# Quarter-array products in one group per turn, selection and feed-forward as two table-driven generators with a PSUM bank each, results summed in the same turn

## The chip, the cores and the metric

One Trainium2 chip, one core of it. The metric is the device time of the program in microseconds; smaller is better. TensorE is called PE here, its weight loads PEld, VectorE DVE, ScalarE ACT, GpSimd POOL, and SyncE, which issues most of the transfers, SP.

## The reference

First a recurrence over 768 steps for 4 batches and 8 heads of 48 (`r`, `k`, `v`, `w` are fp32):

```python
for t in range(S):
    cur = np.einsum('bhd,bhe->bhde', u[None] * kt, vt)
    y[:, :, t] = np.einsum('bhd,bhde->bhe', rt, state + cur)
    state = wt[:, :, :, None] * state + np.einsum('bhd,bhe->bhde', kt, vt)
```

Then, on `x` = `y` with the heads side by side (4 x 768 x 384), in each batch the 128 rows with the highest score go through a two-layer network and are added back:

```python
scores = np.einsum('bsd,d->bs', x, w_gate)
for b in range(B):
    top_idx = np.argpartition(-scores[b], capacity)[:capacity]
    xe = x[b, top_idx]
    ye = np.maximum(xe @ w1, 0.0) @ w2          # 384 -> 1024 -> 384
    g = 1.0 / (1.0 + np.exp(-scores[b, top_idx]))
    out[b, top_idx] = x[b, top_idx] + g[:, None] * ye
```

## The kernel before

The steps of a batch are cut into 6 chunks of 128, so there are 24 chunks, numbered n = 0 to 23, and the order of all instructions is written out by hand: a loop of 28 **turns**, n = -4 to 23. Each engine runs its instructions in the order in which the code names them. A turn works on several chunks at different depths: it loads chunk n+7 (L526), takes the logarithm of `w` of chunk n+4 (`lnw`), its running sums by two 128x128 triangular matmuls (`sums`, `later_sums`), scales `k` and `r` of chunk n+3 (`scaled`), transposes chunk n+2 (`turned` for "K" and for "R"), forms the 64x64 scores and the state's growth of chunk n+1 (`scores`, `fresh`, then `masked` and `states` on DVE), and finishes chunk n (`from_state`, `from_chunk`). `result`, which adds the finished PSUM tile to `vo`, multiplies with `w_gate` and stores `x`, is called for n-1 at the start of the turn.

Two kinds of matmul alternate on PE. `from_state`, `scores`, `fresh` and `from_chunk` use quarters of the array (64 rows by 64 columns); `turned`, `sums`, `later_sums` and everything of the second part use the whole array. fp32 operands go through PE in more than one pass, so 16 quarter matmuls show as x32 in the trace.

PSUM has eight banks: four for the two tiles `ps_p` (one for even, one for odd chunks), three that rotate through `turned` K, `turned` R, `sums` and `later_sums` (pool `psR`), one for the second part (pool `psM`). `from_chunk(n)` writes columns that `from_state(n)` wrote from other rows of the array; it therefore waits for an ACT instruction that comes after `from_state`: the copy of `turned` R's bank (L317), and in the last two turns, where there is none, a small copy `seen` (L306).

The second part is one generator, `mixture(b)`, of 28 pieces: scores of the batch spread to all partitions (`ps_e`, `every`), six comparisons on DVE (`ahead`), counts by matmul (`ps_r`), `rank`, `pick`, row numbers (`ps_i`, `idx`), the gather of 128 rows of `x` from DRAM by POOL (`xe`), its transposes (`ps_x`, `xeT`), the gate, then eight pieces of the first layer (`ps_h`; after every fourth an ACT `Relu` to `hid`), eight of the second (`ps_f`), `ye` and a scatter by POOL. `mixture(b)` is begun in turn 6(b+1) and advanced by 5, 5, 5, 4, 5 and 4 pieces in that turn and the five after it (L479), at three places of each turn (L540, L549, L551). That of the last batch runs behind the loop (L553). The gather reads rows that `result` stored, so it needs the batch's last store.

`x` has three buffers, so `result(n)` waits until the store of chunk n-3 has landed. SP issues the loads, the weights of the second part (one piece per turn from turn 0 to 6), the stores and a small transfer `all` (L165) in one queue.

## Time and profile before

| | |
|---|---|
| median of 3 runs | 261.3 us (260.32 to 262.85) |
| the profiled execution's own time | 257.75 us |
| its span | 256.0 us |
| busy PE / PEld / DVE / ACT / POOL | 206.2 / 151.3 / 127.7 / 89.6 / 91.3 us |
| moved by DMA | 29.36 MB, mean 115 GB/s |
| first sums that need loaded chunk 4 (turn 0) | start at 22.5 us |
| turn 12 begins (K transposes of chunk 14) | 118.72 us |
| `x` of the last chunk | 219.14 us |

Busy time of PE is no measure of its work by itself: matmuls overlap, and one at half clock counts double. What counts is the distance from one group's start to the next group's start. Times in rows are from the span's start. The granted clock is given as a share of 2.4 GHz.

### The profile page before, as it was taken

How to read it: one execution, taken by the hardware profiler on the slowest of the kernel's cores; microseconds unless marked ns; L12 is line 12 of the kernel's file. 1: busy time of each engine (PE TensorE's matmuls, PEld its weight loads, DVE VectorE, ACT ScalarE, POOL GpSimd, SP SyncE). 2: the span in 40 equal slices, each digit the busy share in tenths (PEclk: the TensorE clock that was granted, in tenths of full speed). 3: DMA queues.
4: the chain of work that ended last, by engine and by line, in shares of the span. 5: the costliest groups of instructions: out<-in, count | busy, mean ns of one | idle time of the engine just before them, and what ended most of it. 6: DMA issues, size and time to landing. Idle time of an engine off the chain costs nothing.

```text
span 256.0 us, 8427 instructions
## 1 busy us (share of the span) xinstructions
PE 206.2 (81%) x3634; PEld 151.3 (59%) x3634; DVE 127.7 (50%) x330; ACT 89.6 (35%) x215; POOL 91.3 (36%) x113
## 2 busy tenths in 40 slices
PE   3786999869869499999878999999768999328760
PEld 1353777646646288667556876766548886117630
DVE  6471567535784075236795643437975331641010
ACT  3773465515632124543631455146311210100100
POOL 3370676324551424442655154417453120110010
PEclk9996799988995599999995999999975999955995
DMA  7998999989899974557558325001120000110001
GB/s 143 204 190 164 196 223 213 202 209 218 199 213 212 224 177 78 109 131 157 124 113 200 66 66 124 31 3 64 34 65 3 33 33 33 61 31 0 0 0 44
DMA packets 108540, 29.36 MB, mean 115 GB/s; under 512 B 103376, under 2 KB 107728, under 8 KB 108496
## 3 DMA queue, kind: packets, MB, share of 16 engines
q1 hardware_dynamic: 107984, 27.18, 48.5%
q0 software_dynamic: 512, 1.57, 2.0%
q8 instruction: 30, 0.49, 0.8%
q14 instruction: 14, 0.11, 0.2%
HBM read 23.20 MB, written 5.51 MB: 112 GB/s over the span
## 4 chain that ended last, share of the span: by engine, by line
PE 59%; DMA 13%; DVE 10%; SPq 7%; issue 6%; ACT 1%; POOL 1%; POOLq 0%; DVEq 0%; ACTq 0%
PE ps_h L443 11%; PE ps_f L453 9%; PE ps_p L310 7%; PE ps_x L152 6%; DMA out_dram<-x 6%; SPq L105 6%; PE ps_t L217 6%; PE ps_l L172 5%; PE ps_p L233 5%; DMA xe<-out_dram,idx 5%; PE ps_p L249 4%; PE ps_p L292 4%; DVE ahead L361 3%; DVE sc L261 2%; DMA w<-in_w_dram 2%
## 5 line engine op out<-in xcount | busy, mean ns | idle before, releaser
L261 DVE TENSOR_TENSOR sc<-ps_p,mask 128x512 f32<-128x512 f32 x24 | 16.6, 692 | 67.9 <-PE ps_p L249 67.9
L183 POOL TENSOR_TENSOR rk<-r,k 128x384 f32<-128x384 f32 x24 | 24.0, 998 | 52.9 <-DVE r_buf L207 52.9
L152 PE MATMUL ps_x<-lw,tri 128*128 128x384 f32 x48 | 25.6, 619 | 7.7 <-ACT lw L135 7.7
L219 ACT COPY Kt<-ps_t 128x512 f32<-128x512 f32 x24 | 14.0, 584 | 46.6 <-PE ps_t L217 42.0
L443 PE MATMUL ps_h<-xeT,w 128*128 128x128 f32 x192 | 29.0, 307 | 1.5 <-ACT hid L448 0.9
L281 POOL TENSOR_TENSOR s<-mid,all_buf 128x192 f32<-128x192 f32 x20 | 12.8, 640 | 45.6 <-issue 19.4
L310 PE MATMUL ps_p<-v,sc 64*64 64x48 f32 x768 | 29.0, 227 | 0.0
L310 PEld LDWEIGHTS ps_p<-v,sc 64*64 64x64 f32 x768 | 26.4, 143 | 4.3 <-issue 2.7
L443 PEld LDWEIGHTS ps_h<-xeT,w 128*128 128x128 f32 x192 | 26.5, 216 | 4.0 <-ACT hid L448 1.2
L453 PE MATMUL ps_f<-w,hid 128*128 128x384 f32 x64 | 24.4, 507 | 0.9 <-ACT hid L448 0.7
L184 POOL TENSOR_TENSOR rk<-rk,u_bc 128x384 f32<-128x384 f32 x24 | 24.0, 1000 | 2.7 <-DMA u_bc<-in_u_dram 0.9
L233 PE MATMUL ps_p<-Rt,Kt 48*64 48x64 f32 x768 | 18.1, 237 | 6.2 <-DVE x L326 6.2
L154 ACT ACTIVATE rise<-ps_x 128x384 f32<-128x384 f32 x24 | 11.8, 491 | 30.3 <-PE ps_x L152 26.6
L172 PE MATMUL ps_l<-lw,tri_s 128*128 128x384 f32 x48 | 22.1, 547 | 0.0
L198 POOL TENSOR_TENSOR vo<-v,own 128x384 f32<-128x384 f32 x24 | 21.2, 884 | 2.3 <-DVE x L326 2.3
L233 PEld LDWEIGHTS ps_p<-Rt,Kt 48*64 48x64 f32 x768 | 14.7, 145 | 10.9 <-DVE x L326 7.4
L249 PEld LDWEIGHTS ps_p<-v,k_buf 64*48 64x48 f32 x704 | 11.7, 130 | 13.6 <-issue 10.7
L219 ACT COPY Rt<-ps_t 128x512 f32<-128x512 f32 x24 | 14.1, 586 | 15.5 <-PE ps_t L217 15.5
L326 DVE TENSOR_TENSOR x<-ps_p,vo 128x384 f32<-128x384 f32 x24 | 13.3, 553 | 11.6 <-DMA out_dram<-x 5.8
L292 PE MATMUL ps_p<-s,Rt 48*64 48x48 f32 x704 | 17.3, 231 | 1.0 <-DVE mid L279 0.9
L361 DVE SCALAR_TENSOR_TENSOR ahead<-every,score,behind 128x768 bf16<-128x768 f32 (+5 forms) x24 | 17.5, 770 | 1.2 <-ACT every L351 1.2
L292 PEld LDWEIGHTS ps_p<-s,Rt 48*64 48x64 f32 x704 | 14.3, 143 | 5.8 <-issue 4.2
(78 smaller groups left out, 290.9 us busy)
## 6 DMA issues: line engine op xcount, KB each, us to landing
w<-in_w_dram SPq DMA_DIRECT2D x24, 192.0 KB, 4.0
k<-in_k_dram SPq DMA_DIRECT2D x24, 192.0 KB, 4.1
r<-in_r_dram SPq DMA_DIRECT2D x24, 192.0 KB, 3.9
v<-in_v_dram SPq DMA_DIRECT2D x24, 192.0 KB, 3.8
out_dram<-x SPq DMA_DIRECT2D x24, 192.0 KB, 2.8
w<-in_moe_w_dram SPq DMA_DIRECT2D x3, 512.0 KB, 5.2
w<-in_moe_w_dram SPq DMA_DIRECT2D x4, 384.0 KB, 4.8
all_buf<-line_buf SPq DMA_DIRECT2D x20, 2.0 KB, 3.2
```

Source lines behind the costliest of these rows:

```text
L152: nc.tensor.matmul(ps[:, 0:C], tri, t["lw"], start=True, stop=True)
L172: nc.tensor.matmul(ps[:, 0:C], tri_s, t.pop("lw"), start=True, stop=True)
L183: sync(nc.gpsimd.tensor_mul(rk, t.pop("r"), t.pop("k")), t["scaled"], "one port")
L184: nc.gpsimd.tensor_mul(rk, rk, u_bc)
L219: after[n - 2] = nc.scalar.copy(out=t[name + "t"], in_=ps)
L233: nc.tensor.matmul(P[half(sub), par, j * HB:(j + 1) * HB], t["Kt"][half(par, D), j, half(sub)], t["Rt"][half(par, D), j, half(sub)], start ...
L249: nc.tensor.matmul(t["P"][half(par, D), sub, SC + j * D:SC + (j + 1) * D], t["K"][half(sub), 2 * j + par, 0:D], t["v"][half(sub), 2 * j + ...
L292: nc.tensor.matmul(t["P"][half(sub), par, j * D:(j + 1) * D], t["Rt"][half(par, D), j, half(sub)], t["s1" if sub else "s0"][half(par, D), ...
L310: ins = nc.tensor.matmul(t["P"][half(sub), par, j * D:(j + 1) * D], t["sc"][half(sub), par, j, :], t["v"][half(sub), 2 * j + par, :], star ...
L361: nc.vector.scalar_tensor_tensor(out=ahead[:, c, lo:S], in0=every[:, lo:S], scalar=score[:, b, c:c + 1], in1=behind[:, 0:S - lo], op0=ALU. ...
L443: nc.tensor.matmul(ps[:, q, :], w1[:, dc, (f0 + q) * L:(f0 + q + 1) * L], xeT[:, dc, :], start=(dc == 0), stop=(dc == NDC - 1),)
L453: nc.tensor.matmul(ps, hid[:, fc, :], w2[:, fc, :], start=(fc == 0), stop=(fc == NFC - 1))
```

## The change

It does five things.

1. In each turn the four quarter groups stand together, at the turn's start: `from_state(n)`, `scores(n+1)`, `fresh(n+1)`, `from_chunk(n)`; then `masked`, `states` and `result(n)`. The whole-array work follows: a part of the second part, `turned` K and R, `sums`, a part, `later_sums`, a part.
2. `result(n)` is called in turn n, not in turn n+1, so each store is issued one turn earlier.
3. `from_chunk` waits for a `seen` copy in every turn. The copy stands in ACT's queue behind `lnw(n+4)` and ahead of the copies of `turned`.
4. `psR` has two banks, `psM` two tags with one bank each: "m" for selection, "f" for the network.
5. `mixture` is split into `select(b)` (11 pieces; the last comparison goes with the one before it, and `rank` with `pick`) and `forward(b)` (16 pieces). A table names for each of a batch's six turns, at three places, how many pieces of which run. `select(b)` runs in turns 6(b+1) to 6(b+1)+3, `forward(b)` from turn 6(b+1)+4 on for six turns. So the last ten pieces of `forward(2)` and both generators of the last batch stand behind the loop.

```diff
-    psR = ctx.enter_context(tc.tile_pool(name="psR", bufs=3, space=PSUM))
+    psR = ctx.enter_context(tc.tile_pool(name="psR", bufs=2, space=PSUM))
@@ turned
-        after[n - 2] = nc.scalar.copy(out=t[name + "t"], in_=ps)
+        nc.scalar.copy(out=t[name + "t"], in_=ps)
@@ from_state, at its end
+        seen = lev.tile([L, 2], FP32, tag="seen", name="seen")
+        nc.scalar.copy(out=seen, in_=t["P"][:, :, YW - 1])
@@ from_chunk
-        if n not in after:
-            seen = lev.tile([L, 2], FP32, tag="seen", name="seen")
-            nc.scalar.copy(out=seen, in_=t["P"][:, :, YW - 1])
...
-                    if n in after:
-                        sync(ins, after.pop(n), "other rows of the array in the same bank")
@@
-    def mixture(b):
+    chosen = {}
+
+    def select(b):
...
-            yield
+            if c != NCH - 2:
+                yield
...
         nc.vector.tensor_add(rank, ps, rank)
-        yield
...
                 op=ALU.is_equal,
             )
+            yield
...
+            chosen.setdefault(b, []).append((n, rows, where, xe, xeT, gate))
             yield
-
+            if len(groups) > 1:
+                yield from forward(b)
+
+    def forward(b):
+
+        for n, rows, where, xe, xeT, gate in chosen.pop(b, ()):
             hid = mod.tile([L, NFC, L], FP32, name="hid")
             for f0 in range(0, NFC, 4):
-                ps = psM.tile([L, 4, L], FP32, tag="m", name="ps_h")
+                ps = psM.tile([L, 4, L], FP32, tag="f", name="ps_h")
...
-            ps = psM.tile([L, C], FP32, tag="m", name="ps_f")
+            ps = psM.tile([L, C], FP32, tag="f", name="ps_f")
@@
-    per_turn = [5, 5, 5, 4, 5, 4]
+    plan = [
+        ("sf", "sf", "ss"), ("f", "ssf", "sf"), ("sf", "f", "s"),
...
+    plan_forward = 4 * NCH // 6
+    steps = dict(s=iter(()), f=iter(()))
+
+    def mix(what):
+
+        for x in what:
+            next(steps[x], None)
@@ the loop
-            result(n - 1)
-            if n > 0 and chunks[n][1] == 0:
-                mixing = run(mixing, mixture(chunks[n][0] - 1))
-            pieces = per_turn[chunks[n][1]] if n >= NCH else 0
             lnw(n + 4)
-            turned(n + 2, "K")
             from_state(n)
-            turned(n + 2, "R")
             scores(n + 1)
-            sums(n + 4)
-            mix(pieces // 3)
-            later_sums(n + 4)
+            fresh(n + 1)
+            from_chunk(n)
+            masked(n + 1)
+            states(n + 1)
+            result(n)
             scaled(n + 3)
             own_products(n + 3)
+            own_values(n + 1)
             own_sum(n + 2)
-            fresh(n + 1)
-            masked(n + 1)
-            own_values(n + 1)
-            states(n + 1)
-            mix(pieces // 3)
-            from_chunk(n)
-            mix(pieces - 2 * (pieces // 3))
-        result(N - 1)
-        mixing = run(mixing, mixture(B - 1))
-        mix(1000)
+            parts = ("", "", "")
+            if n >= NCH:
+                b, j = n // NCH - 1, n % NCH
+                parts = plan[j * len(plan) // NCH]
+                if j == 0:
+                    steps["s"] = run(steps["s"], select(b))
+                if j == plan_forward:
+                    steps["f"] = run(steps["f"], forward(b))
+            mix(parts[0])
+            turned(n + 2, "K")
+            turned(n + 2, "R")
+            sums(n + 4)
+            mix(parts[1])
+            later_sums(n + 4)
+            mix(parts[2])
+        steps["s"] = run(steps["s"], select(B - 1))
+        mix("ssfsfsfsfsfsffsfff" + 4 * "s" + 1000 * "f")
+        mix(1000 * "s")
+        steps["f"] = forward(B - 1)
+        mix(1000 * "f")
```

In the listings below, rows of the kernel before have its line numbers and rows of the changed kernel its own (a few lower or higher for the same step). First PE in turn 12, the first of the third batch's chunks; before:

```order
L217 MATMUL ps_t<-ident,k_buf_86 128x128 x4
L292 MATMUL ps_p_94<-s_1829,Rt 64x48 x8
L217 MATMUL ps_t<-ident,r_buf_90 128x128 x4
L233 MATMUL ps_p_95<-Rt,Kt 64x64 x16
L152 MATMUL ps_x<-lw,tri 128x384
L348 MATMUL ps_e<-ident,score 128x128 x3
L172 MATMUL ps_l<-lw,tri_s 128x384
L249 MATMUL ps_p_95<-v,k_buf_85 48x48 x16
L348 MATMUL ps_e<-ident,score 128x128 x3
L310 MATMUL ps_p_94<-v,sc 64x48 x16
```

and with the change:

```order
L291 MATMUL ps_p_94<-s_1812,Rt 64x48 x8
L232 MATMUL ps_p_95<-Rt,Kt 64x64 x16
L248 MATMUL ps_p_95<-v,k_buf_85 48x48 x16
L308 MATMUL ps_p_94<-v,sc 64x48 x16
L346 MATMUL ps_e<-ident,score 128x128 x3
L448 MATMUL ps_h<-xeT,w_80 128x128 x3
L216 MATMUL ps_t<-ident,k_buf_86 128x128 x4
L216 MATMUL ps_t<-ident,r_buf_90 128x128 x4
L151 MATMUL ps_x<-lw,tri 128x384
L346 MATMUL ps_e<-ident,score 128x128 x3
L448 MATMUL ps_h<-xeT,w_80 128x128 x3
L171 MATMUL ps_l<-lw,tri_s 128x384
```

The four products into `ps_p` (state, scores, fresh, chunk) have moved into one run; K, R and `sums` now follow each other with nothing between; and pieces of the first batch's network (`ps_h`) stand in this turn.

Second, DVE around `pick` of the first batch, where turn 8 begins; before:

```order
L261 TENSOR_TENSOR sc<-ps_p_94,mask 128x512
L276 TENSOR_TENSOR s_1268<-ps_p_94,s_1141 128x192
L279 TENSOR_TENSOR mid<-ps_p_94,s_1268 128x192
L361 SCALAR_TENSOR_TENSOR ahead,won<-every,score,behind 128x256
L361 SCALAR_TENSOR_TENSOR ahead,won<-every,score,behind 128x128
L375 TENSOR_TENSOR rank<-behind_n,won 128x6
L376 TENSOR_TENSOR rank<-ps_r,rank 128x6
L385 TENSOR_TENSOR pick<-slots,rank 128x768
L395 TENSOR_SCALAR idx<-ps_i 128x1
L326 TENSOR_TENSOR x<-ps_p_95,vo 128x2x4x48
```

and with the change, in turn 8:

```order
L260 TENSOR_TENSOR sc<-ps_p_95,mask 128x512
L275 TENSOR_TENSOR s_1391<-ps_p_95,s_1269 128x192
L278 TENSOR_TENSOR mid<-ps_p_95,s_1391 128x192
L322 TENSOR_TENSOR x<-ps_p_94,vo 128x2x4x48
L328 ISA scr,score<-x,wg_bc 128x384
L206 TENSOR_TENSOR k_buf_87<-k,e 128x8x48
L206 TENSOR_TENSOR r_buf_90<-r,rise 128x8x48
L190 TENSOR_REDUCE own<-rk 128x8
L374 TENSOR_TENSOR rank<-behind_n,won 128x6
L375 TENSOR_TENSOR rank<-ps_r,rank 128x6
L383 TENSOR_TENSOR pick<-slots,rank 128x768
L394 TENSOR_SCALAR idx<-ps_i 128x1
```

`x`, which waits for the store of three chunks earlier, has moved from behind `idx` to ahead of `rank` and `pick`.

Third, PE behind the last chunk's `from_chunk` (the first row); before:

```order
L310 MATMUL ps_p_95<-v,sc 64x48 x16
L453 MATMUL ps_f<-w_81,hid 128x384 x2
L348 MATMUL ps_e<-ident,score 128x128 x6
L370 LDWEIGHTS ahead
L370 MATMUL ps_r<-ones,ahead 128x1
```

and with the change:

```order
L308 MATMUL ps_p_95<-v,sc 64x48 x16
L448 MATMUL ps_h<-xeT,w_80 128x128 x9
L346 MATMUL ps_e<-ident,score 128x128 x6
L448 MATMUL ps_h<-xeT,w_80 128x128 x6
L458 MATMUL ps_f<-w_81,hid 128x384 x5
L369 LDWEIGHTS ahead
L369 MATMUL ps_r<-ones,ahead 128x1
```

Ten more pieces of the third batch's network stand behind the last chunk (one `ps_h` piece is three matmuls, one `ps_f` piece one); the rows shown end at `ps_r`, and three further `ps_f` follow it, ahead of `ps_i`.

## Rows read from the trace of the kernel before

**Rows 1.** Windows: length; busy PE, PEld, DVE, ACT, POOL; PE clock; DMA share, GB/s
```profile
22.50:60.50 38.00, 34.37 (x752) 24.75 (x752) 19.88 (x46) 19.46 (x47) 19.49 (x23) 0.88 0.96 211
60.50:118.70 58.20, 50.52 (x912) 36.90 (x909) 30.18 (x78) 21.96 (x53) 21.68 (x25) 0.88 0.75 164
118.70:219.10 100.40, 90.70 (x1721) 68.75 (x1719) 56.29 (x144) 33.51 (x80) 38.32 (x42) 0.92 0.29 70
```

**Rows 2.** Timeline, PE, turn 10: start, length, what, idle before it
```profile
110.43 0.60 PE L217 MATMUL ps_t<-ident,k_buf 128*128 128x128 f32 x4
110.96 0.68 PE L292 MATMUL ps_p<-s,Rt 48*64 48x48 f32 x32
111.57 0.66 PE L217 MATMUL ps_t<-ident,r_buf 128*128 128x128 f32 x4
...
113.53 0.81 PE L453 MATMUL ps_f<-w,hid 128*128 128x384 f32 x2
114.18 0.81 PE L172 MATMUL ps_l<-lw,tri_s 128*128 128x384 f32 x2
114.92 0.57 PE L249 MATMUL ps_p<-v,k_buf 64*48 64x48 f32 x32
115.42 0.91 PE L453 MATMUL ps_f<-w,hid 128*128 128x384 f32 x2
116.26 1.14 PE L310 MATMUL ps_p<-v,sc 64*64 64x48 f32 x32
117.33 1.56 PE L453 MATMUL ps_f<-w,hid 128*128 128x384 f32 x4
118.72 0.27 PE L217 MATMUL ps_t<-ident,k_buf 128*128 128x128 f32 x1
```

**Rows 3.** Timeline, PE, turn 22: two quarter groups in a row
```profile
207.09 0.68 PE L292 MATMUL ps_p<-s,Rt 48*64 48x48 f32 x32
207.60 0.66 PE L233 MATMUL ps_p<-Rt,Kt 48*64 48x64 f32 x32
```

**Rows 4.** Timeline, ACT in turn 10: the copy of K's bank
```profile
111.07 0.59 ACT L219 COPY Kt<-ps_t 128x512 f32<-128x512 f32 x1 [3.77 <-PE ps_t L217]
```

**Rows 5.** Timeline, turn 3: from `sums` on PE to `lw` on ACT
```profile
41.56 0.91 PE L152 MATMUL ps_x<-lw,tri 128*128 128x384 f32 x2
...
44.15 0.51 ACT L135 ACTIVATE lw<-w 128x384 f32<-128x384 f32 x1
```

**Rows 6.** Timeline, turn 23: the state's products on PE and `seen` on ACT
```profile
213.85 0.68 PE L292 MATMUL ps_p<-s,Rt 48*64 48x48 f32 x32
...
214.60 0.16 ACT L306 COPY seen<-ps_p 128x2 f32<-128x2 f32 x1 [4.79 <-PE ps_p L292]
```

**Rows 7.** Chain that ended last, 40 to 90 us: start, length, what
```profile
49.04 5.65 DMA out_dram<-x
...
54.78 0.57 DVE x L326
...
75.55 0.87 DVE pick L385
76.42 4.55 DMA out_dram<-x
...
```

**Rows 8.** The same chain behind the loop
```profile
219.14 0.56 DVE x L326
...
227.64 3.15 DMA xe<-out_dram,idx
...
232.37 5.00 PE ps_h L443 x24
...
238.09 2.96 PE ps_h L443 x24
...
248.09 1.01 POOL out_dram L462
```

**Rows 9.** Windows: turn 14's first 6 us; columns as in rows 1
```profile
135.30:141.30 6.00, 6.00 (x82) 4.41 (x80) 2.66 (x7) 1.34 (x3) 3.84 (x4) 0.52 0.87 196
```

More of the change, by code (lines that the diff above doesn't have):

```diff
@@ L94 @@
     work = {n: {} for n in range(N)}
-    after = {}
     def load(n, names="wkrv"):
@@ L309, in from_chunk @@
                 for sub in (0, 1):
-                    ins = nc.tensor.matmul(
+                    nc.tensor.matmul(
                         t["P"][half(sub), par, j * D:(j + 1) * D],
@@ L471, in run @@
             yield from g
-    mixing = iter(())
-    def mix(n):
-        for _ in range(n):
-            next(mixing, None)
-    per_turn = [5, 5, 5, 4, 5, 4]
+    plan = [
+        ("sf", "sf", "ss"), ("f", "ssf", "sf"), ("sf", "f", "s"),
+        ("f", "ff", "ss"), ("f", "f", "f"), ("f", "f", "f"),
+    ]
+    plan_forward = 4 * NCH // 6
[3 more added lines that the diff above has]
+            next(steps[x], None)
     AHEAD = 7
@@ L603, in general @@
                 )
-            for _ in mixture(b):
+            for _ in run(select(b), forward(b)):
                 pass
```

## The prediction

> **What bounds the kernel now.** I read the windows by stage first [rows 1]. Up to 60 us the transfers are the limit: their share is 0.96 at 211 GB/s. From 60.5 to 118.7 us they still take 0.75, and PE is busy for 50.5 of 58.2 us at a clock of 0.88. From 118.7 to 219.1 us they fall to 0.29, PE is busy for 90.7 of 100.4 us, and nothing else is near its limit (DVE 56.3). So PE's order sets the long third stage, and the transfers set the first. Behind 219.14 us comes a chain of small steps to the end at 256.0.
>
> Then the chain of waits in the second stage [rows 7]. The store issued at 49.04 us (chunk 1's) lands 5.65 us later, and only then does `x` of chunk 4 start, at 54.78: the three buffers of `x`. The last store of batch 0, issued at 76.42 right behind `pick`, lands at 80.97, and the first gather needs it. The stores are late because SP issues them in one queue with the loads: chunk 1's and chunk 5's are 27.4 us apart, 6.85 us for each turn.
>
> Last, PE inside a turn, by distances between starts. Turn 10 takes 8.29 us [rows 2], without a pause. It changes between quarters and the whole array four times there and back, and that can be priced: one `ps_f` piece takes 0.65 us between whole-array groups (113.53 to 114.18) and 0.84 between two quarter groups (115.42 to 116.26), so 0.19 goes there; the state's products take 0.61 before a whole-array group (110.96 to 111.57) and 0.51 before `scores` [rows 3], another 0.10. A round trip costs 0.29 us.
>
> **The grouped products.** Turn 10 has four round trips and four pieces of the second part; with the change one round trip and three pieces: 8.29 - 3 x 0.29 - 0.65 = 6.77 us.
>
> **Two banks in `psR`.** `sums` now needs the bank of K, so it waits for the ACT copy of K. That copy starts 0.64 us after K's first transpose and takes 0.59 [rows 2, 4], so `sums` can start 1.23 us after it. Between them stands only R: K's 0.53 [rows 2] holds about 0.09 of a change to quarters, so K and R take 0.88. PE pauses 0.35, with the signal 0.4 us, in each turn. The bounds are 0 (ACT takes K up faster) and 1.0 (`later_sums` waits for R's copy as well, another 0.59). Queued behind `sums` is all of PE; the mixed turn becomes 7.2 us.
>
> **`seen` in every turn.** `seen` ends 0.91 us after the state's first product [rows 6]. `scores` and `fresh` lie beside that: 0.51 + 0.51 + about 0.4 = 1.4 us pass before `from_chunk`. So the copy itself is hidden where ACT is free. Where a turn has no network pieces ACT is not: from the start of `sums` to that of `lw` pass 2.59 us, then 0.51 and 0.16 for `lw` and `seen` [rows 5, 6], 3.26 in all; from `from_chunk` to the next `sums` pass 1.07 [rows 2] + 1.23. A quiet turn is then 5.6 us long, set by ACT, and `from_chunk` is late, with `result` behind it. Quiet turns gain nothing. In mixed turns two pieces of 0.65 behind `sums` cover it; without that cover each would lose up to 0.5.
>
> **Stores one turn earlier.** Chunk 5's store goes out one round earlier, 76.42 - 6.85, plus about 0.9 for one more 0.2 MB store ahead of it at 211 GB/s: 70.5 us, landing 4.55 later at 75.1. Turn 8 would begin near 69 (turn 1 at about 29, which is 22.5 plus `from_chunk`, transposes and sums at half clock, an estimate; then seven quiet turns of 5.6 to 6.2). It has `result(8)`, which waits for exactly this store. Queued behind that `x` on DVE now stand `scr`, two scalings, `own`, `rank` and `pick`: five at about 0.57 [rows 7], then 0.4 for `rank` and 0.87 for `pick`: 79.2 us. `ps_i` on PE, last in the turn, waits for it, so turn 9 begins at about 79.6. The old wait of PE for the gather is gone (a whole turn lies between it and its transposes); this is what takes its place. Turn 9 is quiet, 5.6; turns 10 and 11 take 7.2 each: turn 12 at 99.6, and with 1.4 for a clock that falls in the pause of about 3 us (ahead of turn 14 the like left 6.0 us at 0.52, some 2.9 us lost [rows 9]; I take half) at 101, against 118.72 [rows 2]. Bounds: 96 (the pause doesn't arise) to 107 (the store is not earlier).
>
> **Turns 12 to 23.** Eight turns at 7.2 = 57.6, and 0.8 for selection's matmuls in turns 14 and 15 (by the four transposes' 0.44, twice). The waits for the counts of selection and their half-clock stretches (one is [rows 9]) fall away, because comparisons, counts, `pick` and gather now stand a part or a turn apart. Turn 20 has no sums but waits for `pick`: 7.2. Turn 21: 7.2 - 1.3 - 0.4 + 0.4 = 5.9. Turn 22 has no K and R either: 4.6. In turn 23 `x` comes after 0.91 + 1.07 + 0.25 = 2.2. In all 78.3 us, so the last `x` stands at 179.3. Before it took 100.4 [rows 1, 8]; of the 22 saved, some 6.5 are the ten pieces moved behind the loop.
>
> **Behind the loop.** Before, the gather starts 8.5 us after the last `x` and the end is at 256.0, 36.9 after it [rows 8]. Now 13 network pieces stand on PE ahead of `ps_i`: five at 0.74 (2.96 for four) and eight at 0.65, 8.9 us. After pieces four and eight PE waits for the ReLU, 0.72 each (237.37 to 238.09). With 1.5 for the two spreads of the scores and 0.8 for counts and row numbers this is 12.6, more than DVE's comparisons, which run beneath; then `ye` (0.6) and the scatter's issue on POOL (1.01) go ahead of the gather: 14.3. The end moves from 36.9 to 42.7 behind the last `x`. Bounds: 2.5 (only the first three pieces count) to 9 later. The new pieces don't keep PE busy through the gather, so the cold 5.00 [rows 8] stays.
>
> **Sum.** 101 + 78.3 + 42.7 = 222 us of span; the profiled execution has 1.75 around its span: 223.8. The median of the runs is 3.55 above that execution, so 227 us.
>
> **Rivals.** (a) ACT's hand-offs cost more: both banks are awaited and `seen` stands behind a ReLU; 0.8 more in each of 18 turns, 14 us: 241. For it: three waits on ACT in each turn where one was. Against: ACT is busy for 33.5 of 100.4 us [rows 1]. (b) The transfers hold the first two stages: turn 12 at 110, 236 us. For it: the 0.96 [rows 1]. Against: the round earlier is a matter of order in SP's queue, not of speed. (c) The pause in turn 8 doesn't come and the end is only 3 us later: 5 + 3 less, 219; with a hidden copy of K, 216. (d) Slower: the pauses of 0.4 us and the two banks make PE's clock fall in the mixed turns. At half clock 24 passes take 5.00 for 2.96 [rows 8], 1.69 times, so a turn takes 12.2, 5 us more; the 34 us gained are lost when 7 of 18 mixed turns run so, and all 18 give 317. Against: over the third stage, with all its changes of mode, the clock is 0.92 [rows 1], and the low stretch of [rows 9] stands behind a turn in which PE waited for the counts and for `pick`, far longer than 0.4 us. The Trainium skill (TensorE: Matmul & The Clock Gate, "A second HAM failure mode: psum-queue depth-cycling") tells of a kernel that cycled through PSUM banks, paused briefly between groups, and had its clock go back and forth; by that rule (d) would hold. The trace shows the low clock behind longer waits (0.52 in [rows 9]).
>
> **How the numbers follow.** Forecast 0.62 (219 to 234), (a) 0.14, (b) 0.10, (c) 0.09, (d) 0.03, and 0.02 that gains and new waits cancel. The bounds: turn 12 by -5 and +6, `sums` by -4 and +6 over the mixed turns, the end by -3 and +3; not all on one side at once: 215 to 242. This takes in (a), (b) and (c), and leaves out about 0.12. One percent is 2.6 us, about what a measurement can tell. Faster by over that: 0.95, within it 0.02, slower 0.03.
>
> **What would show it.** Right: one change to quarters in each turn and 7.0 to 7.4 us from state to state in turns 16 to 19; `sums` waiting for the copy of K for 0.3 to 0.5; `seen` ahead of `from_chunk` only in quiet turns; `x` of chunk 8 released by a store near 75 us, and PE waiting for `pick` behind it; turn 12 near 101, the last `x` near 179, the last gather 14 us later. Wrong: mixed turns over 8 us (ACT), turn 12 behind 107 (transfers), a granted clock under 0.8 between 100 and 175 us, or a gather that starts within 10 us.

## The result, and the profile after

The changed kernel takes 241.24 us (median of 4 runs, 239.45 to 242.19), the kernel before, beside it, 260.81 (259.81 to 262.85): ratio 0.923, interval 0.915 to 0.932. The forecast was 227, its range 215 to 242. The direction held and the time lies just inside the range, but 14 us of the gain that I had worked out are missing. The profiled execution took 239.45 us, its span is 237.5.

The stages first, as in [rows 1] (length; busy PE, PEld, DVE, ACT, POOL; PE clock; DMA share, GB/s). The bounds are the starts of turns 1, 7 and 12 and the last `x`.

```profile
28.64:66.29 37.65, 31.90 (x815) 24.44 (x815) 23.19 (x53) 19.65 (x55) 19.12 (x23) 1.00 0.91 201
66.29:110.46 44.17, 34.38 (x751) 27.60 (x750) 32.21 (x73) 18.69 (x52) 23.72 (x26) 0.92 0.88 196
110.46:194.26 83.80, 76.57 (x1705) 61.86 (x1705) 59.73 (x140) 33.99 (x91) 38.84 (x43) 0.98 0.36 85
```

PE's clock has risen from 0.92 to 0.98 in the third stage, and PE's busy time there has come down from 90.7 to 76.6 us, of which the ten pieces moved behind the loop are some 6.5. In the middle stage PE is busy for only 34.4 of 44.2 us: there time is lost.

A table of places makes the comparison (starts are those of the turn's first `from_state` product in PE's timeline):

| | forecast | after |
|---|---|---|
| turn 8 begins | 69 | 73.25 |
| turn 9 begins | 79.6 | 87.88 |
| turn 12 begins | 101 | 110.46 |
| turns 16 to 19, each | 7.0 to 7.4 | 7.64, 7.31, 7.18, 7.43 |
| last `x` | 179.3 | 194.26 |
| last gather, behind it | 14.3 | 14.7 |
| end of the span, behind the last `x` | 42.7 | 43.2 |

So 4.2 us are missing up to turn 8, 4.0 in turn 8, 1.2 in turns 9 to 11, 5.5 in turns 12 to 23 and 0.5 behind the loop: 15.4 us of the span. The median is only 14.2 us above its forecast, because it lies 1.8 us above the profiled execution, where the forecast added 3.55.

Timeline of PE in turn 17, a mixed turn without disturbance (start, length, what, idle before it):

```profile
149.28 0.68 PE L291 MATMUL ps_p<-s,Rt 48*64 48x48 f32 x32
149.79 0.66 PE L232 MATMUL ps_p<-Rt,Kt 48*64 48x64 f32 x32
150.27 0.54 PE L248 MATMUL ps_p<-v,k_buf 64*48 64x48 f32 x32
150.62 1.11 PE L308 MATMUL ps_p<-v,sc 64*64 64x48 f32 x32
151.67 0.94 PE L448 MATMUL ps_h<-xeT,w 128*128 128x128 f32 x6
152.44 0.60 PE L216 MATMUL ps_t<-ident,k_buf 128*128 128x128 f32 x4
152.88 0.60 PE L216 MATMUL ps_t<-ident,r_buf 128*128 128x128 f32 x4
153.77 0.91 PE L151 MATMUL ps_x<-lw,tri 128*128 128x384 f32 x2 [0.29 <-ACT Kt L218]
```

The quarter groups follow each other at 0.51, 0.48, 0.35 and 1.05 us, 2.39 in all. In turn 10 of before ([rows 2] and the two rows here) they took 0.61 (state), 0.62 (`scores`), 0.50 (`fresh`) and 1.07 (chunk), 2.80 in all:

```profile
112.16 0.69 PE L233 MATMUL ps_p<-Rt,Kt 48*64 48x64 f32 x32
112.78 0.91 PE L152 MATMUL ps_x<-lw,tri 128*128 128x384 f32 x2
```

The whole-array groups that stood beside quarters (K, R, `later_sums` and one network piece) have become shorter too, by 0.5 us together in the same timelines. With the 0.41 this makes 0.9 us, for a forecast of 3 x 0.29. The pause ahead of `sums` is there as forecast: from R to `sums` pass 0.89 us where K to R takes 0.44. The step on the mixed turn is right.

What is wrong shows in the list of PE's waits from 66 to 194.3 us (what waited, for what: us in all, times, longest):

```profile
PE ps_i L390 <- DVE pick L383: 7.0, 3, 3.2
PE ps_x L151 <- ACT Kt L218: 3.0, 12, 0.3
PE ps_r L369 <- DVE ahead L359: 2.9, 4, 1.0
PE ps_p L232 <- DVE x L322: 2.2, 2, 1.3
```

PE waits for `pick` three times, 2.35 us in turn 8, 1.46 in turn 14 and 3.23 in turn 20. I had counted on the first, on none in turn 14, and on one in turn 20 that fits into 7.2 us.

**Why turn 8 is late.** POOL's timeline in turns 6 and 7:

```profile
70.08 1.08 POOL L280 TENSOR_TENSOR s<-mid,all_buf 128x192 f32<-128x192 f32 x1 [2.81 <-DMA all_buf<-line_buf]
71.12 1.58 POOL L182 TENSOR_TENSOR rk<-r,k 128x384 f32<-128x384 f32 x1
72.78 1.00 POOL L183 TENSOR_TENSOR rk<-rk,u_bc 128x384 f32<-128x384 f32 x1
73.74 0.82 POOL L197 TENSOR_TENSOR vo<-v,own 128x384 f32<-128x384 f32 x1
```

and DVE's:

```profile
74.60 0.56 DVE L322 TENSOR_TENSOR x<-ps_p,vo 128x384 f32<-128x384 f32 x1 [1.49 <-POOL vo L197]
...
79.02 1.20 DVE L359 SCALAR_TENSOR_TENSOR ahead<-every,score,behind 128x256 bf16<-128x256 f32 x1
80.15 0.08 DVE L359 DVE_READ_ACCUMULATOR ahead<-every,score,behind 128x1 f32 x1
80.15 0.90 DVE L359 SCALAR_TENSOR_TENSOR ahead<-every,score,behind 128x128 bf16<-128x128 f32 x1
...
82.24 0.55 DVE L322 TENSOR_TENSOR x<-ps_p,vo 128x384 f32<-128x384 f32 x1
```

The product `s` (the code's `s0`, here that of chunk 8), which the change put ahead of `rk` on POOL, waits for the small transfer `all`. Behind it stand rk (`r` times `k`), rk*u and `vo` (`v` times `own`, the sum of rk*u by head); `x` needs `vo`; and all of DVE's work of the turn stands behind `x`. The first row is `x` of chunk 7, the last `x` of chunk 8, with no wait ahead of it. The last comparison (128x128) takes 0.90 us here; behind the loop, with POOL idle, the same one takes 0.35.

**Why turn 14 is late.** DVE and POOL in that turn:

```profile
130.56 0.54 DVE L190 TENSOR_REDUCE own<-rk 128x8 f32<-128x384 f32 x1
131.03 0.71 DVE L374 TENSOR_TENSOR rank<-behind_n,won 128x6 f32<-128x6 f32 x1
131.84 0.17 DVE L375 TENSOR_TENSOR rank<-ps_r,rank 128x6 f32<-128x6 f32 x1
132.04 1.56 DVE L383 TENSOR_TENSOR pick<-slots,rank 128x768 bf16<-128x768 f32 x1
```

```profile
130.72 1.00 POOL L182 TENSOR_TENSOR rk<-r,k 128x384 f32<-128x384 f32 x1 [1.44 <-DVE r_buf L206]
131.80 0.99 POOL L183 TENSOR_TENSOR rk<-rk,u_bc 128x384 f32<-128x384 f32 x1
132.75 1.54 POOL L197 TENSOR_TENSOR vo<-v,own 128x384 f32<-128x384 f32 x1
134.50 1.04 POOL L403 DMA_INDIRECT xe<-out_dram,idx  x1 [0.21 <-DVE idx L394]
```

The subtraction for `rank` works on six columns and takes 0.71 us: it ends at 131.74, just when POOL's rk (130.72 + 1.00 = 131.72) is done. The addition that follows, of the same size but with an operand in PSUM, takes 0.17. `pick` ends 0.81 us after rk*u ends (132.79), and `vo`, which began at 132.75, ends 0.69 after `pick` and takes 1.54 instead of 0.82. Alone `pick` takes 0.96 us and `vo` 0.82, so to within 0.15 us each looks as if it had begun only when the other engine's instruction had ended: the two engines take turns, one whole instruction at a time.

### The profile page after: what moved, and what is told of

The parts are those of the page before. It is cut to its first block, busy times and chain, and to the rows that moved or that the text cites. A ratio compares the mean times of both kernels' runs of the same rounds, so it can differ in the third digit from the quotient of the medians.

```text
span 237.5 us, 8471 instructions
## 1 busy us (share of the span) xinstructions
PE 187.6 (79%) x3634; PEld 145.0 (61%) x3634; DVE 135.5 (57%) x330; ACT 90.5 (38%) x237; POOL 93.7 (39%) x113
## 3 DMA queue, kind: packets, MB, share of 16 engines
HBM read 23.20 MB, written 5.51 MB: 121 GB/s over the span
## 4 chain that ended last, share of the span: by engine, by line
PE 36%; DVE 18%; issue 14%; SPq 10%; ACT 7%; DMA 5%; POOL 5%; DVEq 0%; POOLq 0%; ACTq 0%
SPq L104 9%; PE ps_h L448 8%; PE ps_p L308 6%; DVE ahead L359 5%; PE ps_x L151 5%; DMA all_buf<-line_buf 4%; PE ps_f L458 3%; PE ps_p L291 3%; ACT Kt L218 3%; PE ps_p L232 3%; PE ps_t L216 3%; PE ps_l L171 2%; PE ps_p L248 2%; DVE pick L383 2%; DVE x L322 2%
## 5 line engine op out<-in xcount | busy, mean ns | idle before, releaser
L182 POOL TENSOR_TENSOR rk<-r,k 128x384 f32<-128x384 f32 x24 | 25.0, 1041 | 34.5 <-DVE r_buf L206 34.5
L308 PE MATMUL ps_p<-v,sc 64*64 64x48 f32 x768 | 30.0, 229 | 8.5 <-ACT seen L299 5.2
L280 POOL TENSOR_TENSOR s<-mid,all_buf 128x192 f32<-128x192 f32 x20 | 11.4, 571 | 57.2 <-DMA all_buf<-line_buf 20.1
L151 PE MATMUL ps_x<-lw,tri 128*128 128x384 f32 x48 | 24.2, 589 | 10.0 <-ACT lw L134 5.3
L359 DVE SCALAR_TENSOR_TENSOR ahead<-every,score,behind 128x768 bf16<-128x768 f32 (+5 forms) x24 | 21.6, 951 | 7.6 <-ACT every L349 7.6
L197 POOL TENSOR_TENSOR vo<-v,own 128x384 f32<-128x384 f32 x24 | 22.8, 950 | 0.0
L467 POOL DMA_INDIRECT out_dram<-ye,idx x4 | 4.3, 1078 | 40.3 <-DVE total L573 19.5
L232 PE MATMUL ps_p<-Rt,Kt 48*64 48x64 f32 x768 | 17.7, 228 | 2.5 <-DVE x L322 2.5
L151 PEld LDWEIGHTS ps_x<-lw,tri 128*128 128x128 f32 x48 | 7.9, 206 | 16.3 <-ACT Kt L218 9.8
L206 DVE TENSOR_TENSOR k_buf<-k,e 128x384 f32<-128x384 f32 x24 | 14.5, 602 | 4.6 <-ACT e L173 4.6
L160 ACT ACTIVATE line_buf<-ps_x 1x384 f32<-1x384 f32 x20 | 17.0, 849 | 0.0
```

The lines of the kernel that those rows point to most:

```text
L151: nc.tensor.matmul(ps[:, 0:C], tri, t["lw"], start=True, stop=True)
L182: sync(nc.gpsimd.tensor_mul(rk, t.pop("r"), t.pop("k")), t["scaled"], "one port")
L197: nc.gpsimd.tensor_mul(t["vo"], t["v"], t.pop("own").to_broadcast([L, H, D]))
L232: nc.tensor.matmul(P[half(sub), par, j * HB:(j + 1) * HB], t["Kt"][half(par, D), j, half(sub)], t["Rt"][half(par, D), j, half(sub)], start ...
L308: nc.tensor.matmul(t["P"][half(sub), par, j * D:(j + 1) * D], t["sc"][half(sub), par, j, :], t["v"][half(sub), 2 * j + par, :], start=(sub ...
L359: nc.vector.scalar_tensor_tensor(out=ahead[:, c, lo:S], in0=every[:, lo:S], scalar=score[:, b, c:c + 1], in1=behind[:, 0:S - lo], op0=ALU. ...
```

## The experiments

Two theories came out of this. **S**: POOL's order, with the late `all`, holds `vo`, `x` and the selection in turns 6 to 8. **C**: DVE instructions whose two inputs lie in SBUF are held while POOL multiplies. Against them stand the prediction's own rivals: the transfers set the first two stages (**T**), and ACT's hand-offs cost more than I gave them.

**1. The product for `s0` last on POOL, as before the change.**

```diff
-            s0 = ... nc.gpsimd.tensor_mul(s0, mid, ...)   # in states(n + 1)
             own_values(n + 1)
+            decayed(n + 1)                                # the same product
```

> The product for s0 stands last in each turn on POOL, behind rk, rk*u and vo, as it did before the change; nothing else is altered. Theory S (in turns 6 to 8 POOL stands at s0, which waits for a late transfer of `all`, so vo, x and selection on DVE are late): turn 9 starts near 83 us instead of 87.9, turn 12 near 106 instead of 110.5, ratio about 0.905. Rival T (the first two stages are paced by the bytes moved, and the wait of POOL lies beside that): turn 12 within 1.5 us of 110.5, ratio about 0.92 as with the whole change.

Measured: 238.39 us, ratio 0.918 (0.913 to 0.923). Turn 9 begins at 82.9, turn 12 at 106.2, the last `x` stands at 192.15. Turn 7 takes 5.63 instead of 6.96, turn 8 12.56 instead of 14.63. Run 6, whose order up to turn 22 is the change's own, tells how much of this is S: there turn 7 takes 5.64 too, turn 8 14.62, and turn 12 begins at 109.5. So the gain of 2.1 us in turn 8 is the edit's, and the one in turn 7 may as well be the difference between two executions. From turn 7's start to turn 12's pass 41.5 us here, 43.3 in run 6 and 44.2 in the change. Turns 14, 15 and 20 got longer (9.30, 9.02 and 9.30; the gather now stands behind `s0` on POOL), which gives 2 us back. S holds for 2 to 3 us in these turns; the other 1.6 us by which turn 12 is earlier were there when turn 7 began. The whole time moves little, and its interval overlaps the change's.

**2. The weights of the second part later.**

```diff
-            if n >= 0 and n < len(weights):
-                to, of = weights[n]
+            if n in when:                  # when = [5, 6, 7, 8, 9, 10, 11]
+                to, of = weights[when.index(n)]
```

> The seven weight transfers (3.1 MB) are issued in turns 5 to 11 instead of 0 to 6; the order of the compute engines is unaltered. Rival T (bytes pace the first turns): turn 8 starts near 67 us instead of 73.3, turn 12 near 103, ratio about 0.90. Theory S (only the place of `all` in SP's queue matters): turn 8 stays near 73, but `all` lands in time, turn 8 takes 10 us instead of 14.6, turn 12 near 106, ratio about 0.905. If neither: turn 12 stays at 110.

Measured: 237.03 us, ratio 0.909 (0.902 to 0.915). Turn 8 begins at 71.9, not at 67, though the DMA share from turn 1 up to there has fallen from 0.92 (204 GB/s) to 0.86 (178); turns 7 and 8 take 5.65 and 12.03 us; turn 12 begins at 106.5. Turns 1 to 6 are no shorter (38.5 us for 37.7). So the weights' bytes don't set the first stage's turns: T falls, as far as moving these seven transfers can test it. What the weights did was to stand ahead of `all` in SP's queue: that of chunk 8 now lands at 62.2 us instead of 69.9, POOL doesn't wait in turn 6, and `x` no longer waits for `vo`. That is S by another way.

**3. `rank` and `pick` ahead of the scalings.**

```diff
+            mix(parts[0])
             scaled(n + 3)
             own_products(n + 3)
             own_values(n + 1)
             own_sum(n + 2)
...
-            mix(parts[0])
```

> On DVE the first part of a turn's selection work (which is `rank` and `pick` in turns 8, 14 and 20) stands ahead of the two scalings and the `own` sum, so also ahead of POOL's rk, which waits for the scalings. Theory C (`pick` is late because it stands behind DVE's other work and takes 1.56 us instead of 0.96 beside POOL's rk): `pick` takes 0.96, PE's waits for it (1.5 us in turn 14, 3.2 in turn 20, 2.3 in turn 8) shrink under 0.5, turns 14 and 20 take 7.3 us or less instead of 8.8, turn 21 6.2 instead of 7.2; ratio about 0.90 to 0.905. Rival (the counts on PE come too late for `pick` anyway): turns 14 and 20 shorten by under 0.7 us, ratio over 0.915.

DVE's timeline in turn 14 of this kernel:

```profile
126.02 0.16 DVE L374 TENSOR_TENSOR rank<-behind_n,won 128x6 f32<-128x6 f32 x1
126.28 0.16 DVE L375 TENSOR_TENSOR rank<-ps_r,rank 128x6 f32<-128x6 f32 x1
126.48 0.96 DVE L383 TENSOR_TENSOR pick<-slots,rank 128x768 bf16<-128x768 f32 x1
```

Measured: 236.41 us (233.80 to 238.82) beside 259.91 (259.18 to 263.42); the runs spread too far for an interval. `pick` takes 0.96 in all batches, turn 14 7.19 instead of 8.83, turn 20 6.25 instead of 8.80: C holds in these places, and more of turn 20 came back than I expected. But turn 21 now ends with a wait of 1.97 us for the gather (7.88 us instead of 7.23), and turn 22 runs at a clock of 0.56 (7.69 instead of 4.68). The wait moved on.

**4. Network pieces between R and `sums`.**

```diff
-            sums(n + 4)
             mix(parts[1])
+            sums(n + 4)
             later_sums(n + 4)
```

> The middle part of the turn's second-part pieces stands between the transposes of R and `sums`, instead of behind `sums`, so that `sums` no longer waits for the copy of K in turns with pieces there. Theory (the pause of 0.4 us per mixed turn is a cost of the two banks): turns 16 to 19 take 7.0 us instead of 7.2 to 7.6, some 16 turns x 0.35 = 5 us in all, ratio about 0.905. Rival (ACT then comes later to lw and `seen`, so the pause moves to the products of the chunk): turns 16 to 19 within 0.15 us, ratio within 0.01 of 0.923.

PE in turn 17 of this kernel, where `sums` (L151) has no wait any more:

```profile
148.76 0.60 PE L216 MATMUL ps_t<-ident,r_buf 128*128 128x128 f32 x4
149.20 0.91 PE L448 MATMUL ps_h<-xeT,w 128*128 128x128 f32 x6
149.94 0.81 PE L151 MATMUL ps_x<-lw,tri 128*128 128x384 f32 x2
```

Measured: 236.73 us, ratio 0.910 (0.903 to 0.918). Turns 16 to 19 take 7.28, 6.83, 6.68 and 7.08 instead of 7.64, 7.31, 7.18 and 7.43: the pause for K's copy cost 0.35 to 0.5 us per mixed turn, as the prediction had it, and it was avoidable. At the products of the chunk little of it came back: in these four turns PE waits for `seen` twice, 0.5 us in all. The ratio by itself can't be told from the change's (their intervals touch); the turns can.

**5. Scalings and `rk` at the turn's end.** The strongest test of C that keeps all the work:

```diff
-            scaled(n + 3)
-            own_products(n + 3)
             own_values(n + 1)
-            own_sum(n + 2)
...
             mix(parts[2])
+            scaled(n + 3)
+            own_products(n + 3)
+            own_sum(n + 2)
```

> The two scalings, POOL's rk and rk*u and DVE's `own` sum stand at the end of each turn, behind the turn's selection work; POOL's order becomes s0, vo, rk. Theory C (DVE work that reads only SBUF is slowed or held while POOL multiplies; the work that reads PSUM is not): POOL's rk now runs beside DVE's PSUM work, the comparisons take 1.02, 0.88, 0.75, 0.61, 0.48, 0.34 us in every batch, `pick` 0.96, turn 14 about 7.2, turn 20 about 6.3, turn 8 under 12; ratio about 0.895. Rival (the late rk makes `own`, vo and x late in every turn): turns 16 to 19 over 7.8 us, ratio 0.92 or more.

Measured: 229.44 us, ratio 0.889 (0.882 to 0.897). Turns 7 and 8 take 15.3 us together instead of 21.6 (8 alone 7.05), turn 14 7.22, turn 20 7.23 (I had 6.3), and turns 16 to 19 are as before (7.28, 7.31, 7.18, 7.41), so the late rk makes nothing late there. Comparisons and `pick`, the rows of DVE's groups (count, busy us, mean ns), of the change and of this kernel:

```profile
L359 DVE SCALAR_TENSOR_TENSOR ahead<-every,score,behind 128x768 bf16<-128x768 f32 (+5 forms) x24 | 21.6, 951 | 7.6 <-ACT every L349 7.6
L383 DVE TENSOR_TENSOR pick<-slots,rank 128x768 bf16<-128x768 f32 x4 | 5.6, 1409 | 0.1
```

```profile
L359 DVE SCALAR_TENSOR_TENSOR ahead<-every,score,behind 128x768 bf16<-128x768 f32 (+5 forms) x24 | 17.3, 771 | 12.9 <-ACT every L349 12.9
L383 DVE TENSOR_TENSOR pick<-slots,rank 128x768 bf16<-128x768 f32 x4 | 3.8, 958 | 0.1
```

The mean comparison falls from 951 to 771 ns, short of the 680 that the six lengths in the expectation give: some still meet POOL.

**6. The order behind the loop.**

```diff
+            if n == N - 1:
+                parts = ("ff", "", "")
...
-        mix("ssfsfsfsfsfsffsfff" + 4 * "s" + 1000 * "f")
+        mix(7 * "s" + 6 * "f" + "s" + "ff" + "s" + 3 * "f" + 2 * "s" + 1000 * "f")
```

> Only the order behind the loop is altered: the spreads of the last scores stand behind two network pieces instead of three, the counts behind six more instead of seven, the row numbers and the gather behind two more, and the last three network pieces with `ye` and the scatter of the third batch behind the gather. Theory (those pieces delay the last gather, as the sum of the prediction says): the gather starts 10 us behind the last x instead of 14.7, the end is 39 us behind it instead of 43.2, ratio about 0.907. Rival (the comparisons on DVE set the gather anyway): gather within 1 us of 14.7, ratio within 0.005 of 0.923.

Measured: 233.34 us, ratio 0.902 (0.891 to 0.912). The gather starts 11.2 us behind the last `x` (205.49 against 194.28; I had 10), the span ends 36.8 behind it. That is 6.4 us earlier, of which the gather gives 3.5. Most of the rest is the clock. PE of the change, then of this kernel:

```profile
212.31 0.88 PE L411 MATMUL ps_x<-ident,xe 128*128 128x128 f32 x3 [5.47 <-DMA xe<-out_dram,idx]
213.75 5.03 PE L448 MATMUL ps_h<-xeT,w 128*128 128x128 f32 x24 [0.57 <-ACT xeT L413]
```

```profile
208.77 0.52 PE L411 MATMUL ps_x<-ident,xe 128*128 128x128 f32 x3 [1.77 <-DMA xe<-out_dram,idx]
209.86 2.94 PE L448 MATMUL ps_h<-xeT,w 128*128 128x128 f32 x24 [0.57 <-ACT xeT L413]
```

With three network pieces on PE between the row numbers and the transposes of the gathered rows, PE waits 1.77 us instead of 5.47, and the next 24 passes run in 2.94 instead of 5.03 (granted clock 1.00 for 0.56).

**7. The results' sum a turn later again** (and with it the store).

```diff
+            result(n - 1)
             lnw(n + 4)
...
             states(n + 1)
-            result(n)
```

> The results' sum and the store are undone alone: chunk n's sum is called at the start of turn n+1 again. Theory (the earlier store carries a part of the gain, since x of three chunks later waits for it): turn 8 starts 3 us or more later than 73.3, turn 12 later than 114, ratio 0.94 or more. Rival (turn 8 is held by POOL and the selection on DVE, the store is landed in time anyway): turn 12 within 2 us of 110.5, ratio within 0.01 of 0.923.

Measured: 252.94 us, ratio 0.979 (0.971 to 0.987). Three quarters of the change's gain are gone. PE's wait for `x`, over the whole run:

```profile
PE ps_p L232 <- DVE x L322: 17.7, 14, 3.2
```

`scores(n+1)` (L232) writes the tile that `x` of chunk n-1 reads. Grouped, `scores` comes 0.5 us after the turn's start, and a sum that is called there is not done: 17.7 us of waits against 2.5 with the change.

**8. The store alone a turn later**, the sum where the change put it.

```diff
-        nc.sync.dma_start(out=views[b][b, ...], in_=x)    # in result(n)
+        stores.append((views[b][b, ...], x))
...
+            store()                                       # at the start of turn n + 1
             lnw(n + 4)
```

> The sum x and its score stay in the same turn, only the store of x is issued a turn later. It separates the two halves of what was undone in the run with the late sum (ratio 0.979). Theory (the sum has to come early because the scores of the next turn are written into the PSUM tile that it reads; the store's time matters little): ratio within 0.01 of 0.923, turn 12 within 3 us of 110.5. Rival (the store is what counts, as the prediction had it): ratio 0.95 or more, x waiting for the store of three chunks before.

Measured: 242.67 us, ratio 0.944 (0.930 to 0.957), between the two expectations, and the interval overlaps the change's. The trace shows where a little goes: `x` waits for a store of three chunks before for 6.8 us in turns up to 11 (5.3 us in run 7, none in the change), turn 12 begins at 113.1, and from there on all turns are as in the change. Of what run 7 lost, the place of the sum in the tile's cycle carries the larger part; the store's share is about 3 us by the turns (turns 1 to 6 take 40.6 us for 37.7), and by ratios it can't be told.

**9. One generator again.**

```diff
-                parts = plan[j * len(plan) // NCH]
+                pieces = [5, 5, 5, 4, 5, 4][j]
+                parts = ... "s" in thirds, as before the change
-                    steps["s"] = run(steps["s"], select(b))
+                    steps["s"] = run(steps["s"], select(b), forward(b))
```

> The change with its second part undone: selection and network of a batch run as one generator again, one behind the other, 5, 5, 5, 4, 5 and 4 pieces in six turns; the groups, the same-turn sum and the banks stay. Theory (the two generators carry a third or more of the gain, because comparisons, counts, `pick` and gather stand apart): turns 8, 14 and 20 wait for the counts and the next ones for the gather, the end is 37 us behind the last x instead of 43, ratio 0.95 or more. Rival (the groups and the same-turn sum carry nearly all): ratio under 0.935.

Measured: 278.25 us, ratio 1.081 (1.060 to 1.102): slower than before the change. PE at the end of turn 13:

```profile
140.63 0.28 PE L369 MATMUL ps_r<-ones,ahead 128*128 128x1 bf16 x5 [3.02 <-DVE ahead L359]
...
144.06 0.32 PE L390 MATMUL ps_i<-ids,pick 128*128 128x2 bf16 x6 [1.27 <-DVE pick L383]
148.18 0.88 PE L411 MATMUL ps_x<-ident,xe 128*128 128x128 f32 x3 [3.79 <-DMA xe<-out_dram,idx]
```

Counts, row numbers and gather stand one behind the other at the turn's end, with none of the recurrence's groups left between them, and the clock over turns 7 to 23 is 0.86. Grouping takes away cover as well as changes of mode; with the pieces in the old order and places it doesn't pay. Other tables were not tried.

**10. POOL without rk and rk\*u**, DVE's order as in the change.

```diff
-        rk = t["rk"] = ...
-        sync(nc.gpsimd.tensor_mul(rk, t.pop("r"), t.pop("k")), t["scaled"], "one port")
-        nc.gpsimd.tensor_mul(rk, rk, u_bc)
+        t["rk"] = t.pop("r")
```

> POOL's two multiplies rk and rk*u are left out, so `own` is the sum of r instead of r*k*u; DVE's order is that of the change. Theory C (those multiplies hold DVE's SBUF work beside them): `pick` takes 0.96 instead of 1.56 in turns 8, 14 and 20 though it stands where it stood, the first `rank` step 0.17 instead of 0.71, the comparisons 1.02, 0.88, 0.75, 0.61, 0.48, 0.34; turn 14 about 7.6 instead of 8.8, ratio about 0.90. Rival (DVE's own order makes them long): `pick` stays at 1.56.

Measured: 230.74 us, ratio 0.894 (0.882 to 0.906). `pick` stands where it stood, behind both scalings and the `own` sum:

```profile
125.45 0.15 DVE L373 TENSOR_TENSOR rank<-behind_n,won 128x6 f32<-128x6 f32 x1
125.70 0.17 DVE L374 TENSOR_TENSOR rank<-ps_r,rank 128x6 f32<-128x6 f32 x1
125.90 0.96 DVE L382 TENSOR_TENSOR pick<-slots,rank 128x768 bf16<-128x768 f32 x1
```

0.15 for 0.71 and 0.96 for 1.56, in the same place on DVE: POOL's multiplies are the cause. The first batch's six comparisons take 1.01, 0.88, 0.74, 0.62, 0.48 and 0.35 us, where the change has 1.01, 1.12, 0.74, 1.34, 1.20 and 0.90. Turn 8 takes 10.37 us, turn 14 7.65. This settles C.

**11. Five edits together**: run 5, `vo` first on POOL, run 4, run 2 and run 6.

> Five edits together: the scalings and rk at the turn's end, vo first on POOL, the middle pieces between R and `sums`, the weights in turns 5 to 11, and the order behind the loop. If the causes are separate, the gains add: 4 to 5 us around turns 6 to 9, 5 us at the waits for `pick` (turns 8, 14, 20 and the cold turns behind), 5 us at the pauses for K's copy, 4 us behind the loop: about 222 us, ratio about 0.855. If they share one cause (the time is then set by something else, as the transfers), ratio 0.88 or more.

Measured: 213.96 us, ratio 0.829 (0.823 to 0.836), better than the 222 expected. Turn 8 begins at 69.5, turn 12 at 99.4, the last `x` stands at 174.2, the end 38.2 behind it. The row of the third stage, to be held against the one of the change above:

```profile
99.40:174.20 74.80, 73.03 (x1705) 60.51 (x1705) 55.61 (x141) 33.33 (x93) 39.24 (x44) 1.00 0.54 127
```

PE does the same 1705 matmuls, is busy for 73.0 of 74.8 us, and its clock over this stage is 1.00. Against the change's 0.923, runs 2, 4, 5 and 6 gain 0.014, 0.013, 0.034 and 0.021, 0.082 together; this run gains 0.094, and each interval reaches 0.006 to 0.011 to either side. So the gains add, and no one cause lies behind all of them. `vo` first on POOL was not run by itself.

**12. The same with `seen` ahead of `lw` on ACT.**

```diff
-            lnw(n + 4)
             from_state(n)
+            lnw(n + 4)
```

> The combination of five edits (ratio 0.829) with one more: on ACT the copy `seen` stands ahead of `lw` instead of behind it. Theory (in turns without network pieces the products of the chunk wait for `seen` behind lw, 4.6 us in all in that run): turns 4 to 7 take 5.4 instead of 5.6, the wait for `seen` under 2 us, ratio about 0.82. Rival (lw then comes later and `sums` waits for it, the same time at another place): ratio within 0.005 of 0.829.

Measured: 212.17 us (208.67 to 215.45) beside 260.09 (255.65 to 262.83); too wide to tell from run 11. The mechanism is seen: turns 4 to 7 take 5.18, 5.20, 5.51 and 5.20 instead of 5.61, 5.60, 5.91 and 5.61, and PE's wait for `seen` falls from 4.6 us over the whole run to 0.3. So a quiet turn was set by ACT, as the prediction said. `lw`, which now comes later, costs nothing: `sums` waits for it for 5.3 us in either run.

## Why the prediction was right in part

Right, with its size: **grouped products**, three round trips at 0.29 us, measured 0.9; **two banks** (0.4 us for K's copy, measured 0.35 to 0.5 by run 4); **`seen`**, all but hidden in mixed turns (PE waits for it for 1.3 us in all from 66 to 194.3 us) and setting quiet ones, 5.60 us for a forecast 5.6 (run 12 takes 0.4 off); turns 16 to 19, three of the four within 0.03 us of the range given; **behind the loop**, 43.2 for 42.7, with the cold 5.03 us. Rival (d), the clock that falls through short pauses and the two banks, did not come: over the third stage, with 8 of the 12 short waits for K's copy (at most 0.3 us each), the clock is 0.98. The Trainium skill (TensorE: Matmul & The Clock Gate, "A second HAM failure mode: psum-queue depth-cycling") tells of such a kernel; this trace doesn't show it.

That the time lies inside the range is in part luck. Turn 12 came 3.5 us behind the bound of 107 set for it, and by another cause than the transfers that such a delay was to mean; the 5.5 us in turns 12 to 23 came from waits for `pick`, not from the pause of `sums` to which the range gave 6.

Wrong:

- **"Stores one turn earlier", the place of turn 8.** The step put everything on the store of chunk 5. The store came near its forecast (issued at 72.12 us for 70.5), but it is not what holds turn 8: in the trace `x` of chunk 8, at 82.24 us, waits for no store. It stands behind comparisons on DVE that began late because `x` of chunk 7 waited for `vo`. The prediction named what is queued behind `x` on DVE, but for POOL it followed only the gather and the scatter: that `states` now stands ahead of `own_products` and `own_values` there, so that rk and `vo` queue behind the wait for `all`, appears in no step. From turn 7 to turn 12 run 1 gives back 1.8 to 2.7 us of the 9.5 missing at turn 12, and run 2 3.0 to 3.9 (against run 6 and against the change); in run 5, where `vo` no longer stands behind rk and the comparisons are shorter, turn 12 begins at 103.4.
- **The durations of DVE's work.** `pick` at 0.87 is its share of the chain in [rows 7]; the instruction itself took 1.08 us there and 0.96 in the other batches, and the 0.4 for `rank` stands in no row (before, its two steps took 0.34 to 0.50). In the kernel before rk*u had ended at 73.90, ahead of the first batch's `rank` and `pick` (from 75.08 on). The change moved these behind the scalings, and rk waits for just the scalings. Measured: 1.56 for `pick` and 0.88 for both steps of `rank`. The Trainium skill has this (SBUF — State Buffer, "Who interferes with whom"): a DVE instruction with two inputs in SBUF contends with a GpSimd instruction that reads SBUF, and the port pair that they share is an exclusive lock. The trace agrees: 0.15 us without rk, 0.71 with it, ending as rk ends.
- **Turns 12 to 23**, 83.8 us for 78.3. The sum gave turns 14 and 15 only 0.8 us for the selection's matmuls and turn 20 7.2 with its wait; instead PE waits 1.46 us for `pick` in turn 14 and 3.23 in turn 20, and turn 21 runs at a clock of 0.76. Turn 14 took 8.83 for 7.6, turn 20 8.80 for 7.2, turn 21 7.23 for 5.9: 4.2 of the 5.5 us; runs 3, 5 and 10 each shorten turns 14 and 20.
- **What the same-turn sum is for.** The prediction valued it by the store. Runs 7 and 8 show that its main work is to free the PSUM tile before the grouped `scores` come. Had that been seen, the forecast would not have changed, since the change has both, but its reason would.
- Rival (a) at 241 and (b) at 236 come near the measured time, but by other causes: run 2 shows that bytes don't set the turns, and ACT's waits are of the size forecast. The number is no support for either.

What stays open: in turns 2 and 3 of the change PE stops for 1.08 and 2.08 us in the middle of the 32 products of the chunk, for nothing that the profile shows ("issue"):

```profile
38.05 0.55 PE L308 MATMUL ps_p<-v,sc 64*64 64x48 f32 x12 [1.08 <-issue]
45.16 0.91 PE L308 MATMUL ps_p<-v,sc 64*64 64x48 f32 x25 [2.08 <-issue]
```

They are 3.2 us in all, a part of the 4.2 us missing up to turn 8; the kernel before has none. All twelve runs have such stops at the products of the chunk, 1.5 to 3.6 us together, and in every one the first stands at the same place, ahead of the last 12 of the 32 products in turn 2; in most the second stands ahead of the last 25 in turn 3. So they seem to belong to a place in PE's stream of instructions and not to a partner. No run was aimed at them. Other early differences are not explained either: in the five executions whose order is the same up to turn 6 (the change, runs 3, 4, 6 and 9) turn 1 begins at 27.1 to 29.3 us and turn 6 at 58.3 to 60.0.

## What to carry to other kernels

When an edit moves a step, write down the new queue of every engine that it touches, the helper engines too, and ask of each entry what it waits for and who waits behind it. Take durations of DVE work from rows where the same neighbours run on POOL, or place DVE work that reads PSUM beside POOL's multiplies and work with two SBUF inputs away from them. And grouping work of one kind removes cover: see to it in the same change that each hand-off has other work, some turn earlier or later, to hide under.

## What the runs showed of the hardware

- A six-column subtraction on DVE takes 0.15 us alone and 0.71 beside a POOL multiply; an addition of the same size with one operand in PSUM takes 0.17 either way. `pick` takes 0.96 or 1.56, and POOL's `vo` beside it 1.54 instead of 0.82: whoever comes second waits for the whole instruction.
- PE's clock after a wait: 1.77 us for the gather (run 6) left the next 24 passes at a clock of 1.00, 5.47 us (the change) at 0.56 for the first five us. In run 3 a wait of 1.97 us was followed by 7.7 us at 0.56 (the row below, columns as in [rows 1]), so the length of the last wait alone does not tell.

```profile
180.00:187.70 7.70, 7.70 (x131) 7.48 (x130) 3.41 (x12) 0.84 (x3) 0.81 (x1) 0.56 0.16 55
```

- A 2 KB transfer can hold two engines: the data of `all` of chunk 8 were written by 55.2 us, the transfer was issued at 66.05 behind loads, a weight and a store in SP's queue, and it landed 3.9 us later; POOL, and DVE through `vo`, waited.
